# Moving the transposes of the next-but-one pair's k directly behind the narrow matmuls, in a kernel of kernelized attention and a two-layer mixer

## The chip, the cores and the metric

The kernel runs on one core of a Trainium2 chip. The metric is device time in microseconds (us) of one execution. Before the change it is 1147.09 us, the median of three runs (1145.02 to 1147.52).

## The reference

Inputs are q, k and v (8 batches, 8 heads, 576 rows, 64 columns), w_phi (64 x 128), and for the mixer U (576 x 32), V (32 x 576), w_ch1 (512 x 2048) and w_ch2 (2048 x 512).

```python
def phi(x):
    proj = np.einsum('bhsd,df->bhsf', x, w_phi)
    proj = proj - np.max(np.abs(proj), axis=-1, keepdims=True)
    return np.concatenate([np.exp(proj), np.exp(-proj)], axis=-1)
q_p, k_p = (phi(q), phi(k))
kv = np.einsum('bhsf,bhsd->bhfd', k_p, v)
z = np.sum(k_p, axis=2)
num = np.einsum('bhsf,bhfd->bhsd', q_p, kv)
den = np.einsum('bhsf,bhf->bhs', q_p, z)[..., None] + 1e-06
# x = num / den, with heads side by side: (8, 576, 512)
xt = x.transpose(0, 2, 1)
h = xt @ U @ V
u = x + h.transpose(0, 2, 1)
return u + np.maximum(u @ w_ch1, 0.0) @ w_ch2
```

The weights of the mixer come as 64-bit numbers, and the kernel converts them itself.

## The kernel before, in words

**Work.** Attention goes by pairs: two heads of one batch, 32 pairs (b, j) with j = 0 to 3. The 576 rows are four tiles of 128 and a tail of 64; the tails of the two heads, of k and of q, share tiles of their own. For each pair the kernel loads k, q (`raw`, `t_r`) and v (`vb`, `vt`), transposes k and q on TensorE (PE) into PSUM, copies them from there to SBUF, projects them with w_phi, builds the features (maxima and both exponentials), and then does narrow matmuls: kv = features of k times v with a column of ones (L840, L850), and features of q times kv (L870, L877). After the four pairs of a batch, `Tokens` does U and V (`split`, `down`, `up`), and `Mixer` the two wide layers for 512 rows at a time.

**Precision by splitting.** PE works with fp32r operands that are split in a high and a low part. `stack` (L462) does this for the transposed tiles: ScalarE (ACT) copies a half from PSUM to rows 0 to 63 of the tile (`stack_hi`, L468), and VectorE (DVE) writes the remainder to rows 64 to 127 (`stack_lo`, L471). So each transposed tile needs two copies and two subtractions before it is usable, and its PSUM bank is full until then. The narrow matmuls are plain fp32 and use half of the array's columns at a time.

**Filling PE.** The mixer's matmuls are cut into chunks of 12 matmuls of 128x512: `hidden` (L1079) into the one bank of the tag "ph", followed by a relu on ACT (L1095) and its remainder on DVE (L1096), and `add` (L1110) into four banks "o". `mix()` issues the next chunk. Chunks are put between the steps of the pairs, so that PE has work while ACT, DVE and GpSimd (POOL) make features.

**Order.** The first seven pairs and most of the first mixer are issued from a list (`ORDER`), on all engines. From the eighth pair on, the function `ordered` is used. There PE's order is the program's, written by hand (`manual_schedule` for the tensor engine alone), and the other engines' queues are ordered by the framework, from its own simulated clock and the program order. Once fixed, every queue runs in order.

**One pair in `ordered`.** While pair n (`cur`) is finished, pair n+1 (`nxt`) makes its features, and pair n+2 (`far`) is loaded and has its k transposed. In order on PE: k tail and first half (`s_k0`), chunk, second half (`s_k1`, L810), chunk, transposes of q of nxt (L732), chunk, the block of narrow matmuls (`narrow`: `s_out` of cur, `s_kv` of nxt), chunk, tail and first half of q (`s_q0`: L822, L823 into pqt, L831, L832 into pq0), chunk, second half (`s_q1`: L831, L832 into pq1), transposes of k of far (one of the tail, L477, into tT, and four, L732, into T0), and two more chunks. In the last pair of a batch (j = 3) no k is transposed at this place; it is done in `boundary`, between the batches. In j = 1, half of the batch's result is split after the narrow block (`tk.split(0)`, ACT and DVE) and multiplied with U after the transposes (`tk.down(0)`).

**Buffers.** PSUM has eight banks: three with the tag "at" (L145), one "ph", four "o". The "at" banks are taken by pkt, pk, T0, T1, tT, xp0, xp1, kv_ps, pqt, pq0, pq1, pp, vp and pt, whichever comes next, as they come free. In SBUF the transposed tiles live in the pool `att`, which has one buffer for each tag that asks for no more: `tail_T` (L478, for k's tail and q's) and `T` (L735, for k and for q in turn) have one each, feature tiles four. `raw` has two, `t_r` one. A tile's buffer goes to the next tile when all that read or write it is done.

```python
    att = ctx.enter_context(tc.tile_pool(name="att", bufs=1))
    BANKS = {"at": 3, "ph": 1, "o": 4}
    return pT, att.tile([P, 2, SM], F32R, tag="T", name=f"T{n}_{self.nm}")
    self.tail_T = att.tile([P, 2, P], F32R, tag="tail_T", name=f"tail_T{nm}")
```

Of the kernel before, what the change touches and what calls it, by code (L numbers as in the profile page):

```python
# [103 lines left out]
def tile_kernel(  # L104
# [1047 lines left out]
    def mix(n=1):  # L1152
        for _ in range(n):
            if todo:
                fn, f, *ts = todo.pop(0)
                fn(f, *ts)
# [11 lines left out]
    def narrow(nxt, cur, x, xt):  # L1168

        with tc.manual_schedule(engines={nc.tensor.engine}):  # L1170
            cur.s_out(x, xt)
            if nxt is not None:
                nxt.s_kv()
# [108 lines left out]
    def boundary(m, early=None, late=None):  # L1282

        mix(len(todo) - 5)
        if early is not None:
            early(2)
            early(3)
        m.transposes(0)
        mix()
        m.transposes(1)  # L1290
        m.transposes(2)
        mix()
        m.transposes(3)
        mix()
        if early is not None:
            early(NT)
        if late is not None:
            late()
        mix()
        new = m.chunks()  # L1300
        todo.insert(0, new.pop(0))
        todo.extend(new)
        mix()

    def ordered(cur, nxt, x, xt, tk, far):

        for n, (b, j) in list(enumerate(pairs))[ORDERED:]:
            last = j == NPAIR - 1
            if far is None and n + 2 < len(pairs):
                far = Pair(*pairs[n + 2])  # L1310
                far.load_v()

            def do(who, name):
                if who is not None:
                    getattr(who, name)()

            do(nxt, "s_k0")
            mix(2 if j == 0 else 1)
            do(nxt, "s_k1")
            if not last:  # L1320
                mix()
            do(nxt, "transpose_q")
            mix()
            narrow(nxt, cur, x, xt)
            if j == 1:
                tk.split(0)
            if last:
                tk.split(1)
            mix()
            do(nxt, "s_q0")  # L1330
            mix()
            do(nxt, "s_q1")
            if not last:
                do(far, "transpose_k")
                mix()
                if j == 1:
                    tk.down(0)
                mix()
            else:
                mix()  # L1340
                tk.down(1)
                mix()
                tk.up(0)
                tk.up(1)
                mix()
                boundary(Mixer(b, x), tk.up, far.transpose_k if far is not None else None)
                if nxt is not None:
                    if b % 2 == 1:
                        xt = moe.tile([P, C], F32, tag="xt", name=f"xt{b + 1}")
                        nc.vector.memset(xt[ST:P], 0.0)  # L1350
                    x = moe.tile([P, NT, C], F32, tag="x", name=f"x{b + 1}")
                    tk = Tokens(b + 1, x, xt)
            cur, nxt, far = nxt, far, None
        x = moe.tile([P, NT, C], F32, tag="x", name="x_tail")
        nc.sync.dma_start(out=x, in_=u_dram[B])
        boundary(Mixer(B, x))
        mix(len(todo))
# [8 lines left out]
    with tc.manual_schedule(engines={nc.tensor.engine}):  # L1366
        ordered(cur, nxt, x, xt, tk, None)
# [31 lines left out]
```

## Time and profile before

| | |
|---|---|
| median of three runs | 1147.09 us |
| the profiled execution's own time | 1146.92 us |
| its span, first to last instruction | 1145.1 us |
| mean granted clock of TensorE | 0.996 |
| chain that ended last: PE, DVE, DMA, ACT | 91%, 6%, 1%, 1% |
| of it: L1110 (add), L1079 (hidden) | 35%, 33% |
| of it: narrow matmuls L877, L850 | 5%, 5% |

How to read the rows: times are microseconds from the span's start unless marked ns. PE is the matmul, PEld the weight load, which overlaps it; ACT, DVE, POOL and SP are ScalarE, VectorE, GpSimd and the queue that issues DMAs (SPq). L732 is line 732 of the kernel. A row of the timeline has start, duration, engine, line, operation, output and inputs, and how many were merged; in brackets stands how long the engine had been idle and what let it go. A row of a group has the count, the summed time, the mean in ns, and the idle time ahead of it. Matmuls are pipelined: they start every 0.23 us in a chunk although a row shows 0.39 us for one, and their ends are modelled. A window's row has, for each engine, busy us and the number of instructions, then PEclk, the granted clock as a share of full speed.

### The profile page before, as it was taken

The page shows a single profiled execution, that of the slowest core. Times are in us where ns is not written, and L with a number is a line of the kernel's source. Part 1 is how long each engine was busy: PE and PEld are TensorE (multiplying, and loading weights), DVE is VectorE, ACT ScalarE, POOL GpSimd, SP SyncE. Part 2 cuts the span into 40 slices and gives each one's busy share as a digit, 9 for nine tenths or more (in the row PEclk, how much of TensorE's full clock was granted, in tenths as well). Part 3 has the DMA queues.
Part 4 walks back from the last instruction along what each step waited for, and adds up shares of the span by engine and source line. Part 5 has one row for each costly group of instructions (what it writes and reads, how often), then busy time and mean ns, then how long its engine had stood idle before and what let it go on. Part 6 is the DMA issues. An engine that isn't in the chain of part 4 may idle for free.

```text
span 1145.1 us, 22294 instructions
## 1 busy us (share of the span) xinstructions
PE 1124.7 (98%) x9234; PEld 921.2 (80%) x9241; DVE 655.5 (57%) x1355; ACT 525.6 (46%) x1134; POOL 157.4 (14%) x119
## 2 busy tenths in 40 slices
PE   7889999999999999999999999999999999999998
PEld 5775666688888888888888888888888888888886
DVE  7999988856655656655565655665565633112111
ACT  6878876445434544344534544454544521111110
POOL 4321111011111111011201111121101110000000
PEclk9999999999999999999999999999999999999999
DMA  7355533211122112211131112211221005001001
GB/s 195 90 162 174 167 107 121 104 38 32 52 81 69 32 33 76 84 40 33 50 108 32 32 53 73 74 35 32 67 99 32 20 1 171 1 0 38 1 1 37
DMA packets 90532, 75.73 MB, mean 66 GB/s; under 512 B 51648, under 2 KB 76736, under 8 KB 90304
## 3 DMA queue, kind: packets, MB, share of 16 engines
q1 hardware_dynamic: 90112, 73.79, 21.5%
q8 instruction: 73, 1.20, 0.4%
q10 hardware_dynamic: 320, 0.52, 0.1%
q14 instruction: 27, 0.22, 0.1%
HBM read 55.41 MB, written 18.87 MB: 65 GB/s over the span
## 4 chain that ended last, share of the span: by engine, by line
PE 91%; DVE 6%; DMA 1%; ACT 1%; SPq 1%; issue 0%; POOL 0%; DVEq 0%
PE o L1110 35%; PE ph L1079 33%; PE xp L877 5%; PE kv_ps L850 5%; PE pk L810 2%; PE T L732 2%; PE pt L1058 1%; PE pp L969 1%; PE kv_ps L840 1%; PE pq L831 1%; PE xp L870 1%; PE pq L832 1%; PE vp L993 1%; DMA w<-in_moe_w_ch_dram 1%; DVE w_r L240 0%; DVE w_r L243 0%
## 5 line engine op out<-in xcount | busy, mean ns | idle before, releaser
L1079 PE MATMUL ph<-uT_hi,w_hi 128*128 128x512 f32 x576 | 230.9, 401 | 0.0
L1079 PE MATMUL ph<-uT_hi,w_lo 128*128 128x512 f32 x576 | 224.9, 390 | 0.0
L1079 PE MATMUL ph<-uT_lo,w_hi 128*128 128x512 f32 x576 | 224.6, 390 | 0.0
L1096 DVE SCALAR_TENSOR_TENSOR h_lo<-ph,h_hi 128x512 fp32r<-128x512 f32 x128 | 88.1, 689 | 228.8 <-ACT h_hi L1095 228.8
L1110 PE MATMUL o<-w_hi,h_hi 128*128 128x512 f32 x512 | 205.2, 401 | 0.0
L1110 PE MATMUL o<-w_lo,h_hi 128*128 128x512 f32 x512 | 200.1, 391 | 0.0
L1110 PE MATMUL o<-w_hi,h_lo 128*128 128x512 f32 x512 | 200.0, 391 | 0.0
L1095 ACT ACTIVATE h_hi<-ph 128x512 fp32r<-128x512 f32 x128 | 76.5, 598 | 259.1 <-PE ph L1079 258.9
L1079 PEld LDWEIGHTS ph<-uT_hi,w_lo 128*128 128x128 f32 x576 | 108.1, 188 | 23.5
L1079 PEld LDWEIGHTS ph<-uT_hi,w_hi 128*128 128x128 f32 x576 | 108.2, 188 | 22.2 <-issue 0.5
L1079 PEld LDWEIGHTS ph<-uT_lo,w_hi 128*128 128x128 f32 x576 | 108.4, 188 | 21.6 <-issue 0.9
L1110 PEld LDWEIGHTS o<-w_hi,h_lo 128*128 128x128 f32 x512 | 96.1, 188 | 21.0
L1110 PEld LDWEIGHTS o<-w_hi,h_hi 128*128 128x128 f32 x512 | 96.2, 188 | 18.7
L1110 PEld LDWEIGHTS o<-w_lo,h_hi 128*128 128x128 f32 x512 | 96.4, 188 | 17.4
L788 POOL PARTITION_ALL_REDUCE qp_t<-qp_t x24 | 17.8, 740 | 626.8 <-ACT qp_t L787 626.8
L788 POOL PARTITION_ALL_REDUCE qp<-qp x48 | 95.9, 1998 | 32.2 <-ACT qp L787 30.6
L471 DVE TENSOR_TENSOR T<-T,T 64x512 fp32r<-64x512 f32 x96 | 66.2, 689 | 29.6 <-ACT T L468 27.0
L468 ACT CAST T<-T 64x512 fp32r<-64x512 f32 x96 | 55.9, 582 | 36.1 <-PE T L732 19.3
L877 PE MATMUL xp<-kv,qp 128*64 128x65 f32 x2048 | 66.8, 222 | 1.9 <-DVE kv L857 1.5
L850 PE MATMUL kv_ps<-vb,kp 128*64 128x65 f32 x2048 | 66.6, 224 | 0.0
L877 PEld LDWEIGHTS xp<-kv,qp 128*64 128x64 f32 x2048 | 63.1, 138 | 4.1 <-ACT kp L651 2.0
L850 PEld LDWEIGHTS kv_ps<-vb,kp 128*64 128x64 f32 x2048 | 65.7, 140 | 0.0
(156 smaller groups left out, 1564.8 us busy)
## 6 DMA issues: line engine op xcount, KB each, us to landing
w<-in_moe_w_ch_dram SPq DMA_DIRECT2D x32, 512.0 KB, 3.9
raw<-in_q_dram SPq DMA_DIRECT2D x32, 256.0 KB, 2.7
raw<-in_k_dram SPq DMA_DIRECT2D x32, 256.0 KB, 3.0
vb<-in_v_dram SPq DMA_DIRECT2D x64, 128.0 KB, 3.0
u_dram<-x SPq DMA_DIRECT2D x32, 256.0 KB, 2.6
st<-u_dram SPq DMA_DIRECT2D x16, 512.0 KB, 3.8
out_dram<-st SPq DMA_DIRECT2D x32, 256.0 KB, 2.5
t_r<-in_k_dram SPq DMA_DIRECT2D x32, 32.0 KB, 2.2
```

What stands on the lines that cost most here:

```text
L468: nc.scalar.copy(out=dst[0:D], in_=src)
L471: nc.vector.tensor_sub(dst[D:2 * D], src, f32(dst[0:D]))
L732: nc.tensor.transpose(out=pT[:, c * P:(c + 1) * P], in_=self.raw[n][:, c // 2, c % 2, :], identity=ident)
L788: nc.gpsimd.partition_all_reduce(qp[0], qp[1], P, ReduceOp.absmax)
L810: nc.tensor.matmul(pk[:, i, :, :], self.T[0][:, i, cs], w_hl, start=True, stop=True)
L831: nc.tensor.matmul(pq, w_hi, qT, start=True, stop=False)
L850: nc.tensor.matmul(self.kv_v[z * HP:(z + 1) * HP, f, g, :], kp[f][:, i, z * HP:(z + 1) * HP], self.vb[:, g, t, :], start=False, stop=(t == ...
L877: nc.tensor.matmul(xv[zs, c, :], qp[f][:, c * P + z * HP:c * P + (z + 1) * HP], self.kv[:, f, c // 2, :], start=(f == 0), stop=(f == 1), s ...
L1079: nc.tensor.matmul(ph, l[:, c * P:(c + 1) * P], r[:, c, :], start=(n == 0), stop=(n == len(terms) * NCC - 1))
L1095: nc.scalar.activation(out=h_hi, in_=ph, func=AF.Relu)
L1096: nc.vector.scalar_tensor_tensor(out=h_lo, in0=ph, scalar=0.0, in1=f32(h_hi), op0=ALU.max, op1=ALU.subtract)
L1110: nc.tensor.matmul(self.o[t], l[:, cs], r, start=(f == 0 and n == 0), stop=(f == NFC - 1 and n == len(terms) - 1))
```

## The change

In `ordered`, the transposes of `far`'s k are issued directly behind the narrow block instead of behind the second half of q, that is, two chunks earlier, ahead of `s_q0` and `s_q1`. This holds for j = 0, 1 and 2; the last pair of a batch, which has them in `boundary`, is not changed. No instruction is added or left out, and all sizes and buffers stay.

```diff
             do(nxt, "transpose_q")
             mix()
             narrow(nxt, cur, x, xt)
+            if not last:
+                do(far, "transpose_k")
             if j == 1:
                 tk.split(0)
             if last:
@@ -1331,7 +1333,6 @@
             mix()
             do(nxt, "s_q1")
             if not last:
-                do(far, "transpose_k")
                 mix()
                 if j == 1:
                     tk.down(0)
```

## The prediction

> **What bounds the kernel now.** I read the page first, then busy time by windows, then the waits, and then the timeline around one move of the transposes.
>
> ```profile
> span 1145.1 us, 22294 instructions
> PE 1124.7 (98%) x9234; PEld 921.2 (80%) x9241; DVE 655.5 (57%) x1355; ACT 525.6 (46%) x1134; POOL 157.4 (14%) x119
> ```
>
> TensorE (PE) is busy for 98% of the span, so it is the engine to watch. An average can hide a stage with another limit, so the second view is busy time in windows: a gap early on, the stretch behind that gap, and the ordered part.
>
> ```profile
> core 0: us, PE busy (x) PEld busy (x) DVE busy (x) ACT busy (x) POOL busy (x), PEclk, DMA share, GB/s
> 195.60:198.50 2.90, 0.40 (x2) 0.00 (x0) 2.84 (x6) 2.14 (x4) 0.00 (x0) 1.00 0.31 90
> 198.50:203.40 4.90, 4.89 (x9) 2.26 (x10) 4.83 (x9) 2.98 (x5) 0.00 (x0) 0.65 0.76 270
> 221.00:947.00 726.00, 726.00 (x6405) 618.27 (x6404) 418.66 (x877) 335.35 (x751) 107.68 (x69) 1.00 0.17 51
> ```
>
> The change touches only the ordered part, and there (221 to 947 us) PE is busy for 726.00 of 726.00 us at the full granted clock. No other engine sets the end. So only two things count: what an instruction costs in PE's own stream, and whether PE, whose order is written by hand, now meets a wait that it doesn't meet today. Each of either adds directly to the time.
>
> **How often.** Transposes of k are issued 23 times by this function:
>
> ```profile
> L477 PE MATMUL tT<-ident,t_r 128*128 128x128 f32 x23 | 6.2, 270 | 0.0
> ```
>
> Six of these stand in the boundaries (tokens 1 to 6) and do not move. The 17 others move: three pairs in each of tokens 2 to 6, and j = 0 and 1 in token 7, where j = 2 has no next-but-one pair.
>
> **Removed at the old place.** The timeline of PE, first with the transposes behind the second q projection, then one pair later (j = 3), where they do not stand there:
>
> ```profile
> 422.35 0.39 PE L832 MATMUL pq<-T,w_hl 128*128 128x512 f32 x1
> 422.58 0.27 PE L477 MATMUL tT<-ident,t_r 128*128 128x128 f32 x1
> 422.69 0.60 PE L732 MATMUL T<-ident,raw 128*128 128x128 f32 x4
> ...
> 425.88 0.39 PE L1079 MATMUL ph<-uT_hi,w_hi 128*128 128x512 f32 x1
> ```
> ```profile
> 446.86 0.39 PE L832 MATMUL pq<-T,w_hl 128*128 128x512 f32 x1
> ...
> 449.81 0.76 PE L969 MATMUL pp<-xs,u_all 128*128 128x256 f32 x5
> ```
>
> From the last projection matmul to the end of the following chunk of 12 matmuls it is 425.88 − 422.35 = 3.53 us with the five transposes and 449.81 − 446.86 = 2.95 us without. The old place costs 0.58 us each, 17 × 0.58 = 9.9 us.
>
> **Added at the new place.** The trace has transposes directly behind narrow matmuls, early on; beside them stands the place where they will be put:
>
> ```profile
> 67.24 3.44 PE L850 MATMUL kv_ps<-vb,kp 128*64 128x65 f32 x64
> 70.60 1.10 PE L1058 MATMUL pt<-ident,x 128*128 128x128 f32 x8
> ```
> ```profile
> 259.92 2.04 PE L850 MATMUL kv_ps<-vb,kp 128*64 128x65 f32 x64
> 261.89 0.50 PE L1079 MATMUL ph<-uT_hi,w_hi 128*128 128x512 f32 x1
> ...
> 264.76 0.22 PE L822 MATMUL pqt<-tail_T,w_hl 128*128 128x128 f32 x1
> ```
>
> A transpose starts 0.08 us before the modelled end of the narrow block (70.68), a chunk 0.07 us before it (261.96): the way out of the narrow block costs both the same. Eight transposes start within 1.10 − 0.27 = 0.83 us. In the four above, starts are (0.60 − 0.27)/3 = 0.11 apart, so the first gap is 0.17 us and the fifth transpose starts 0.17 + 3 × 0.11 = 0.50 us behind the first. From a fifth transpose (423.02) to the end of the chunk behind it is 425.88 − 423.02 = 2.86 us. The stretch from the narrow block to the tail's q projection so becomes 0.50 + 2.86 = 3.36 us where it is 264.76 − 261.89 = 2.87 us: +0.49 us each, 17 × 0.49 = 8.3 us. The move alone is worth 8.3 − 9.9 = −1.6 us: one change of matmul kind less in each pair.
>
> **The wait that comes with it.** Transposed k needs two PSUM banks (tT, T0) and goes by ScalarE (ACT) and VectorE (DVE) into the SBUF tiles T and tail_T. The pool `att` gives each of these tags one buffer. At the old place the current pair's q has left both. At the new place it has not: T still holds the transposed q, which L831 and L832 read, and tail_T its tail, read by L822 and L823. A new user of a buffer waits for its last reader, as the loads of the raw tiles show in SP's waits:
>
> ```profile
> SPq L434 <- PE T L732: 207.6, 23, 12.2
> ```
>
> So the copies out of T0's bank cannot start before the second q projection, and those out of tT's bank not before the tail's. Only three banks carry the tag "at". Two stay full over the next chunk, and pqt, pq0 and pq1 must share the third. The projections pqt and pq0 stand back to back: pq0 now waits until ACT has copied pqt out. pq1 comes a chunk later and finds a free bank. Today's rows, first a pair with an add chunk in front, then one with a hidden chunk (j = 1):
>
> ```profile
> 418.77 0.28 PE L823 MATMUL pqt<-tail_T,w_hl 128*128 128x128 f32 x1
> 419.09 0.27 ACT L787 COPY qp_t<-pqt 128x128 f32<-128x128 f32 x1 [7.12 <-PE pqt L823]
> 419.17 0.39 PE L832 MATMUL pq<-T,w_hl 128*128 128x512 f32 x1
> ```
> ```profile
> 264.96 0.60 ACT L1095 ACTIVATE h_hi<-ph 128x512 fp32r<-128x512 f32 x1 [2.85 <-PE ph L1079]
> 265.21 0.39 PE L832 MATMUL pq<-T,w_hl 128*128 128x512 f32 x1
> 265.45 0.26 ACT L787 COPY qp_t<-pqt 128x128 f32<-128x128 f32 x1
> ```
>
> And how soon PE starts once another engine lets it go:
>
> ```profile
> 198.03 0.42 DVE L982 TENSOR_TENSOR pst<-pp,pst 32x256 fp32r<-32x256 f32 x1
> 198.51 0.73 PE L993 MATMUL vp<-pst,v_all 128*128 128x512 f32 x2 [2.51 <-DVE pst L982]
> ```
>
> PE starts 198.51 − 198.45 = 0.06 us after the release, and the second matmul starts 0.73 − 0.39 = 0.34 us after the first, since nothing hides the weight load. With an add chunk in front the copy ends at 419.36, so L832 starts at 419.36 + 0.06 + 0.34 = 419.76 instead of 419.17: 0.59 us of stall. With a hidden chunk in front ACT does the relu first, the copy ends at 265.71, and L832 starts at 266.11 instead of 265.21: 0.90 us. Eleven of the 17 pairs (j = 0 and 2) are of the first kind, six (j = 1) of the second: 11 × 0.59 + 6 × 0.90 = 11.9 us.
>
> That is the low end. The tail's stacking becomes ready at the same moment as the pqt copy and stands earlier in the program, so ACT may take its first copy ahead. How ACT's stacking runs today:
>
> ```profile
> 297.84 0.26 ACT L468 CAST tail_T<-tT 64x128 fp32r<-64x128 f32 x1
> 298.00 0.59 ACT L468 CAST T<-T 64x512 fp32r<-64x512 f32 x1
> ...
> 298.24 0.28 DVE L471 TENSOR_TENSOR tail_T<-tT,tail_T 64x128 fp32r<-64x128 f32 x1
> 298.62 0.26 ACT L468 CAST tail_T<-tT 64x128 fp32r<-64x128 f32 x1
> ```
>
> An ACT instruction behind the small copy starts 0.16 us after it (298.00 − 297.84). Put ahead of pqt, that adds 17 × 0.16 = 2.7 us: the high end is 14.6 us. No row says which ACT takes, so I take the middle, 13.2 us.
>
> **What hides the rest.** The banks of xp0 and xp1 should be free when the transposes come: the last DVE read of xp1, in the tightest kind of pair (j = 1), ends at 261.36, the narrow block at 261.96. The bank of kv_ps is free before pqt.
>
> ```profile
> 260.94 0.42 DVE L892 TENSOR_TENSOR x<-xp,den 128x256 f32<-128x256 f32 x1
> ...
> 262.50 0.42 DVE L857 COPY kv<-kv_ps 128x260 f32<-128x260 f32 x1
> ```
>
> T must be full before the next pair's k projection, two chunks (over 5 us) behind pq1. Its stacking still starts at the end of pq1, as today, and two halves of 0.59 and about 0.7 us each fit twice. The transposes issue no DMA, but they free t_r and the raw k buffer, whose next loads are on SP:
>
> ```profile
> 422.88 0.62 SPq L446 DMA_DIRECT2D t_r<-in_k_dram  x1
> 423.60 0.55 SPq L434 DMA_DIRECT2D raw<-in_k_dram  x1
> 424.20 0.62 SPq L446 DMA_DIRECT2D t_r<-in_q_dram  x1
> ```
>
> These would issue some 6 us earlier, among the loads of v, and be needed some 25 us later: nothing. POOL gets q's maxima under a microsecond later, about 20 us before use: nothing.
>
> **The sum**, against the profiled execution's 1146.92 us (span 1145.1 and 1.8 around it; it lies 0.2 us under the median 1147.09): 1146.92 − 1.6 + 13.2 = 1158.5 us. Its own range, by the two ends of the stall, is 1157.2 to 1159.9.
>
> **Rivals.**
> 1. *No wait at pq0 (not slower).* If the stacking could leave the banks within the chunk behind the transposes, which takes a second buffer for T and tail_T, pq0 would find a bank and only the −1.6 us of the move would stay: 1145.3 us. It decides as soon as tT's bank is free before pqt ends. For it: the chunk is 2.86 us long, and ACT is idle (7.12 us in the row of 419.09). Against it: one buffer for each tag. Chance 0.09.
> 2. *pq0 gets tT's bank instead of pqt's.* Then it waits for the whole chain of the tail: copy, subtract, copy, subtract, with starts 0.40 and 0.38 apart in the rows at 297.84, and so 0.40 + 0.38 + 0.40 + 0.28 = 1.46 us in place of a copy of 0.27. The stalls become 1.78 and 2.10 us, in all 32.2: 1146.9 − 1.6 + 32.2 = 1177.5 us. Against it: pqt's bank is free first, whoever goes first on ACT. Chance 0.06.
> 3. *The transposes wait too.* xp1's read has a margin of 0.6 us in the six j = 1 pairs, and there DVE also has the split's subtractions. One such operation ahead costs up to 0.42, 2.5 us in all. If T0 had to take the bank of kv_ps, whose copy ends at 262.92, it would start at 262.98 instead of 261.89 + 0.17: 0.92 × 6 = 5.5 us. 1161 to 1164 us. Chance 0.06.
> 4. *The stalls cost clock.* The gap of 2.51 us before 198.51 was followed by 4.90 us at a granted clock of 0.65, a loss of 0.35 × 4.9 = 1.7 us. If each of the 17 stalls did that: 1158.5 + 29 = 1187.5 us. Against it: PE's weight loads sit idle ahead of the narrow blocks 22 times, 0.35 us on average, and the ordered part has PEclk 1.00.
>
> ```profile
> PEld xp L870 <- issue: 7.6, 22, 0.4
> ```
>
> The stalls are between the two sizes, nearer the small one: chance 0.03. The Trainium skill has this rule ("TensorE: Matmul & The Clock Gate", section "A second HAM failure mode: psum-queue depth-cycling"): waiting on PSUM banks can idle PE briefly and so often that its clock swings between half and full. By that rule the trace agrees for the long gap and not for the short ones.
>
> **How the numbers follow.** The stall at pq0 has 0.76: 1158.5 us. The range must leave out no more than 0.2; without rivals 1, 2 and 4 it leaves out 0.18. Its low end: the stall is 0.59 in all 17 pairs if ACT copies pqt ahead of the relu, 10.0 − 1.6 gives 1155.3, and 0.05 us of misreading each gives 1154. Its high end is rival 3 on top of 1159.9: 1166. A measurement of this kernel can tell about 0.2%, 2.3 us, from no change; rival 1, at −0.14%, lies inside that but for a little. Faster 0.02, same 0.08, slower 0.90.
>
> **What would show it.** In the changed profile: a gap of 0.4 to 1.1 us on PE ahead of L831 in 17 pairs, released by ACT's L787 of qp_t, longer for j = 1; L477 right behind L850; tail_T's L468 behind L823, T's L468 behind the second L832; no new wait at L477 or L732. Wrong it would be if L831 still follows L823 within 0.2 us (rival 1), if the releaser is DVE's L471 (rival 2), if L732 waits (rival 3), or if PEclk falls below 1 in the ordered part (rival 4).

## The result, and the profile after

The changed kernel takes 1158.4 us (median of four runs, 1157.66 to 1159.31) against 1147.01 us for the kernel before in the same session: a ratio of 1.0106, with a 95% interval of 1.0093 to 1.0118. It is slower by 11.4 us. The profiled execution took 1159.31 us. The page after, then the window of the ordered part:

```profile
span 1157.5 us, 22310 instructions
...
PE 1127.6 (97%) x9234; PEld 923.4 (80%) x9241; DVE 661.4 (57%) x1355; ACT 523.6 (45%) x1134; POOL 155.7 (13%) x119
```
```profile
core 0: us, PE busy (x) PEld busy (x) DVE busy (x) ACT busy (x) POOL busy (x), PEclk, DMA share, GB/s
221.00:959.60 738.60, 728.05 (x6406) 619.64 (x6406) 424.49 (x878) 333.45 (x751) 106.73 (x69) 1.00 0.17 50
```

PE has the same number of matmuls as before and the full clock, but it is idle for 738.60 − 728.05 = 10.55 us of a stage in which it had no idle time. The waits of PE, and of its weight loads, say who ended that time:

```profile
PE pq L831 <- ACT qp_t L787: 10.5, 17, 0.8
```
```profile
PEld pq L831 <- ACT qp_t L787: 12.9, 17, 1.0
```

Neither line was there before, and the 17 waits are those of the 17 pairs whose transposes moved. L831 writes pq0, and L787 of qp_t is ACT's copy out of pqt. The idle time on PE understates the wait: in the pair below, L831 starts 0.79 us behind L823 where it was 0.11, but PE counts as idle for 0.51 us only, since the row of L823 covers the rest. Here is one pair with an add chunk in front, PE, ACT and DVE together:

```profile
234.20 0.52 PE L850 MATMUL kv_ps<-vb,kp 128*64 128x65 f32 x12
...
234.65 0.33 PE L477 MATMUL tT<-ident,t_r 128*128 128x128 f32 x1
...
234.81 0.60 PE L732 MATMUL T<-ident,raw 128*128 128x128 f32 x4
...
238.07 0.28 PE L823 MATMUL pqt<-tail_T,w_hl 128*128 128x128 f32 x1
238.38 0.26 ACT L468 CAST tail_T<-tT 64x128 fp32r<-64x128 f32 x1 [7.59 <-PE pqt L823]
238.55 0.26 ACT L787 COPY qp_t<-pqt 128x128 f32<-128x128 f32 x1
238.68 0.28 DVE L471 TENSOR_TENSOR tail_T<-tT,tail_T 64x128 fp32r<-64x128 f32 x1 [3.49 <-ACT tail_T L468]
...
238.86 0.50 PE L831 MATMUL pq<-T,w_hl 128*128 128x512 f32 x1 [0.51 <-ACT qp_t L787]
```

The transposes stand directly behind the narrow block and wait for nothing. ACT had been idle for 7.59 us although the tail has lain transposed in its bank since 235: its copy is let go by L823, the last reader of the old tail_T. ACT then takes the tail's copy ahead of that of pqt, and PE goes on 0.05 us after the end of the second (238.81). The same place in a pair with a hidden chunk in front, where the relu comes first as well:

```profile
265.98 0.28 PE L823 MATMUL pqt<-tail_T,w_hl 128*128 128x128 f32 x1
266.12 0.60 ACT L1095 ACTIVATE h_hi<-ph 128x512 fp32r<-128x512 f32 x1 [3.33 <-PE ph L1079]
266.61 0.25 ACT L468 CAST tail_T<-tT 64x128 fp32r<-64x128 f32 x1
...
266.76 0.27 ACT L787 COPY qp_t<-pqt 128x128 f32<-128x128 f32 x1
267.08 0.19 PEld L831 LDWEIGHTS pq<-T,w_hl 128*128 128x128 f32 x1 [0.96 <-ACT qp_t L787]
267.08 0.50 PE L831 MATMUL pq<-T,w_hl 128*128 128x512 f32 x1 [0.82 <-ACT qp_t L787]
...
267.42 0.40 PE L832 MATMUL pq<-T,w_hl 128*128 128x512 f32 x1
```

From L823 to L832 it is now 267.42 − 265.98 = 1.44 us here and 1.13 us in the other kind (L832 at 239.20), where it was 0.40 in both: stalls of 1.04 and 0.73 us.

**A sharper ruler.** Medians of one kernel scatter by a microsecond or more, and in the profiles most of that lies ahead of the ordered part. There the granted clock is not the same in each: its mean from 0 to 232 us is 0.99 in the profile before, 0.98 in the one after, and from 0.98 to 1.00 in the runs below. So the runs below are compared by the stretch of PE from the kv matmuls that start at about 232 us to the last L877. Before and after, from the timeline and from the line of that group (its first and last start):

```profile
232.18 0.61 PE L840 MATMUL kv_ps<-vt,kp_t 128*64 128x130 f32 x8
```
```profile
L877 PE MATMUL xp<-kv,qp x2048: 220/222/271, 24.7 to 937.4; 128*64 128x65 f32 x187
```
```profile
232.24 0.61 PE L840 MATMUL kv_ps<-vt,kp_t 128*64 128x130 f32 x8
```
```profile
L877 PE MATMUL xp<-kv,qp x2048: 220/222/316, 25.0 to 949.9; 128*64 128x65 f32 x187
```

Before it is 937.4 − 232.2 = 705.2 us, after 949.9 − 232.2 = 717.7 us: +12.5 us. Within a profile the time from one pair's kv matmuls to the next pair's repeats to 0.02 us from batch to batch.

### The profile page after: what moved, and what is told of

Same layout as the page of the kernel before. It is cut to its first block, busy times and chain, and to the rows that moved or that the text cites. A ratio compares the mean times of both kernels' runs of the same rounds, so it can differ in the third digit from the quotient of the medians.

```text
span 1157.5 us, 22310 instructions
## 1 busy us (share of the span) xinstructions
PE 1127.6 (97%) x9234; PEld 923.4 (80%) x9241; DVE 661.4 (57%) x1355; ACT 523.6 (45%) x1134; POOL 155.7 (13%) x119
## 4 chain that ended last, share of the span: by engine, by line
PE 90%; DVE 5%; ACT 2%; DMA 1%; SPq 1%; issue 0%; POOL 0%; DVEq 0%
PE o L1110 34%; PE ph L1079 33%; PE xp L877 5%; PE kv_ps L850 5%; PE pk L810 2%; PE T L732 2%; PE pt L1058 1%; PE pp L969 1%; PE pq L831 1%; PE kv_ps L840 1%; PE xp L870 1%; PE pq L832 1%; PE vp L993 1%; DMA w<-in_moe_w_ch_dram 1%; DVE w_r L243 0%
## 5 line engine op out<-in xcount | busy, mean ns | idle before, releaser
L471 DVE TENSOR_TENSOR T<-T,T 64x512 fp32r<-64x512 f32 x96 | 66.2, 689 | 45.2 <-ACT T L468 43.2
L877 PE MATMUL xp<-kv,qp 128*64 128x65 f32 x2048 | 68.1, 224 | 1.9 <-DVE kv L857 1.5
L877 PEld LDWEIGHTS xp<-kv,qp 128*64 128x64 f32 x2048 | 64.4, 140 | 4.1 <-ACT kp L651 2.0
```

The source lines that it names most:

```text
L471: nc.vector.tensor_sub(dst[D:2 * D], src, f32(dst[0:D]))
L877: nc.tensor.matmul(xv[zs, c, :], qp[f][:, c * P + z * HP:c * P + (z + 1) * HP], self.kv[:, f, c // 2, :], start=(f == 0), stop=(f == 1), s ...
```

## The experiments

Three theories were held against each other. A, that of the prediction: two of the three "at" banks stay full, so pq0 must wait for the copy of pqt. B: the order on ACT is what PE waits for, the tail's copy ahead of that of pqt. C: transposes behind the narrow block are dear in PE's own stream. In the table, the ordered stretch is that of one profile of each kernel, against 705.2 us; the ratio is of the runs' times against those of the kernel before in the same session.

| run | ordered stretch | ratio, 95% interval | waits at pq0 |
|---|---|---|---|
| the change | +12.5 us | 1.0106 (1.0093 to 1.0118) | 17 |
| only the four transposes of T0 moved | −1.3 us | 0.9991 (0.9982 to 0.9999) | none |
| only the tail's transpose moved | −0.9 us | 0.9988 (0.9979 to 0.9997) | none |
| tail stacked later in the program | +10.6 us | 1.0095 (1.0082 to 1.0108) | 17 |
| second buffer for the tail (14 pairs moved) | −1.5 us | 0.9996 (0.9986 to 1.0005) | none |
| moved in j = 1 alone | +5.5 us | 1.0050 (1.0037 to 1.0062) | 6 |
| moved, pqt early | +0.1 us | 1.0013 (1.0003 to 1.0022) | none; 5 waits at pqt |
| pqt early alone | +1.8 us | 1.0032 (1.0021 to 1.0042) | none; 5 waits at pqt |
| moved, pqt early in j = 0, 1, 2 | −2.3 us | 0.9976 (0.9968 to 0.9985) | none |
| pqt early in j = 0, 1, 2 alone | −0.6 us | 0.9991 (0.9982 to 1.0000) | none |

**Only the four transposes of T0 moved.** `transpose_k` is cut in two; the tail's half stays at the old place.

```diff
             narrow(nxt, cur, x, xt)
             if not last:
-                do(far, "transpose_k")
+                do(far, "transpose_k_main")
...
             do(nxt, "s_q1")
             if not last:
+                do(far, "transpose_k_tail")
```

> Only the four transposes of T0 stand behind the narrow block; the tail's one (tT) stays behind the second q projection. Theory A: one bank stays full over the chunk, pqt and pq0 have the two others, no wait at L831. Move alone: old place 0.58 - 4 x 0.11 = 0.14 us left there, 0.49 - 0.11 = 0.38 us added, 0.06 us less for each of 17: -1.0 us against the kernel before. Rival B: the same. Rival C: four fifths of +11.4 stay, +9 us.

The wait is gone (pq0's first matmul starts 0.11 us behind pqt's last in all pairs, as in the kernel before), and the stretch is 1.3 us shorter than before. With one bank full there is one for pqt and one for pq0. This speaks against C, which left 9 us.

**Only the tail's transpose moved.** The two halves change places.

> Only the tail's transpose (tT) stands behind the narrow block; the four of T0 stay behind the second q projection. Theory A: again one bank is full, so no wait at L831, about -1.0 us against the kernel before, though ACT still takes the tail's first copy ahead of that of pqt. Rival B: ACT's order is as in the changed kernel, so the wait stays, 17 stalls of 0.73 or 1.04 us, +13 us. Rival C: a fifth of +11.4, +2.3 us.

The stretch is 0.9 us shorter than before, and this run tells A from B. The row order on ACT is that of the changed kernel, the tail's copy ahead of that of pqt, and yet PE does not wait (the new functions put the lines 12 further down: L835 is L823, L843 is L831, L799 is L787):

```profile
236.75 0.28 PE L835 MATMUL pqt<-tail_T,w_hl 128*128 128x128 f32 x1
...
236.87 0.45 PE L843 MATMUL pq<-T,w_hl 128*128 128x512 f32 x1
...
237.07 0.26 ACT L468 CAST tail_T<-tT 64x128 fp32r<-64x128 f32 x1 [7.14 <-PE pqt L835]
...
237.23 0.26 ACT L799 COPY qp_t<-pqt 128x128 f32<-128x128 f32 x1
```

pq0 starts at 236.87, ahead of both copies. Each half of the move alone is harmless; only both together, which fill two banks, bring the wait. B as the cause is out.

**The tail stacked later in the program.** The transposes stay behind the narrow block, but the calls that copy out of tT and T0 stand behind `s_q0` and `s_q1`.

```diff
             narrow(nxt, cur, x, xt)
             if not last:
-                do(far, "transpose_k")
+                do(far, "transpose_k_pe")
...
             do(nxt, "s_q0")
+            if not last:
+                do(far, "transpose_k_tail")
             mix()
             do(nxt, "s_q1")
             if not last:
+                do(far, "transpose_k_T")
```

> The changed kernel, but the copies out of tT and T0 stand in the program behind the steps s_q0 and s_q1 instead of ahead, so ACT should take the copy of pqt first. Transposes and banks as in the changed kernel. Theory A: pq0 still waits for the copy of pqt, 0.16 us less in each of 17 pairs (0.59 and 0.90 us instead of 0.73 and 1.04): 2.4 to 2.7 us under the changed kernel, +8.9 us over the one before. Rival B: the wait goes, -1.8 us against the kernel before. Rival C: as the changed kernel, +11.4 us.

Lines are 20 further down here (L843 is L823, L807 is L787, L851 and L852 are L831 and L832):

```profile
PE pq L851 <- ACT qp_t L807: 7.9, 17, 0.7
```
```profile
237.87 0.28 PE L843 MATMUL pqt<-tail_T,w_hl 128*128 128x128 f32 x1
238.18 0.27 ACT L807 COPY qp_t<-pqt 128x128 f32<-128x128 f32 x1 [7.59 <-PE pqt L843]
238.34 0.26 ACT L468 CAST tail_T<-tT 64x128 fp32r<-64x128 f32 x1
...
238.50 0.53 PE L851 MATMUL pq<-T,w_hl 128*128 128x512 f32 x1 [0.35 <-ACT qp_t L807]
```

ACT now takes pqt first, and PE still waits 17 times, each time shorter: L851 starts 0.63 us behind L843, where L831 started 0.79 us behind L823. So ACT's order is a part of the price, 0.16 us each, and not the cause. The stretch became shorter by 1.9 us and not by the expected 2.4 to 2.7; the last section comes back to that.

**A second buffer for the tail.** SBUF has no free KB for it in all tokens, but from token 3 on one buffer of the split weights is unused. The pairs of token 2 keep the old place.

```diff
-            self.tail_T = att.tile([P, 2, P], F32R, tag="tail_T", name=f"tail_T{nm}")
+            if self.b > SPLIT and self.par == 1:
+                t = const.tile([P, C], F32R, tag=f"wl{2 * NFC}", name=f"tail_T{nm}")
+                self.tail_T = t[:, 0:2 * P].rearrange("p (a b) -> p a b", a=2)
+            else:
+                self.tail_T = att.tile([P, 2, P], F32R, tag="tail_T", name=f"tail_T{nm}")
```

> From token 3 on, the tails of odd pairs go to a second SBUF buffer, so far's tail can be stacked at once; the 14 pairs of tokens 3 to 7 have the transposes behind the narrow block, the three of token 2 keep the old place. Theory A (banks: two of three stay full, so pq0 waits for the copy of pqt): tT's bank comes free within the chunk, pq0 finds a bank, no wait at L831, and only the gain of the move is left, 14 x -0.11 = -1.5 us: 0.13% below the kernel before. Rival B (ACT's queue: the tail's first copy ahead of that of pqt is what PE waits for): the same, since the tail is stacked earlier. Rival C (transposes behind narrow matmuls are dear in PE's own stream): 14/17 of +11.4 stay, +9.4 us.

The rows of a pair in token 3 show the tail leaving its bank within the chunk (lines are 4 further down: L827 is L823, L835 is L831):

```profile
359.02 0.33 PE L477 MATMUL tT<-ident,t_r 128*128 128x128 f32 x1
...
359.38 0.26 ACT L468 CAST tail_T<-tT 64x128 fp32r<-64x128 f32 x1 [4.22 <-PE tT L477]
...
360.29 0.29 DVE L471 TENSOR_TENSOR tail_T<-tT,tail_T 64x128 fp32r<-64x128 f32 x1 [0.33 <-ACT tail_T L468]
...
362.44 0.28 PE L827 MATMUL pqt<-tail_T,w_hl 128*128 128x128 f32 x1
...
362.56 0.45 PE L835 MATMUL pq<-T,w_hl 128*128 128x512 f32 x1
```

ACT starts on the tail right behind its transpose and no longer waits for pqt, and tT's bank has been read out at 360.58, nearly 2 us before pqt. The stretch is 1.5 us shorter, as A worked it out, with the same transposes at the new place and no wait. So what kept tT's bank full is the one SBUF buffer behind it, and the move alone is worth 0.11 us a pair. T was given no second buffer: here too its copy out of T0 starts only behind the second half of q, so one bank stays full, which does no harm. In the runs' times the gain can't be told from no change.

**Moved in j = 1 alone.** The eleven other pairs keep the old place.

> Only the six pairs with j = 1 have the transposes behind the narrow block, the eleven others keep the old place. Theory A with the relu as part of the price: six stalls of 1.04 us less six times the move's 0.09 = +5.7 us in the ordered part. If all 17 pairs cost the same (12.5 / 17 = 0.74 us each): +4.4 us. If only the add-chunk pairs paid: -0.6 us.

+5.5 us, 0.92 us for each of the six pairs. They cost more than the others, and in their rows above it is the relu that ACT does ahead of the copies, so the relu is a part of the price. The eleven others then paid (12.5 − 5.5) / 11 = 0.64 us each.

**pqt early.** If tail_T is to be free sooner without a second buffer, its last reader has to come sooner. The tail's q projection needs only tail_T, so it can stand a chunk ahead of the narrow block.

```diff
             do(nxt, "transpose_q")
+            do(nxt, "project_q_tail")
             mix()
             narrow(nxt, cur, x, xt)
...
         def s_q0(self):
-            self.project_q_tail()
```

> The changed kernel, and the tail's q projection (pqt) is issued a chunk ahead of the narrow block, behind the transposes of q, instead of right ahead of pq0. No buffer is added. tail_T is then free when far's tail is transposed, so tT's bank empties within the chunk, and pqt's own bank is long free. Theory A: no wait at L831 in any of the 17 pairs, 17 x -0.11 = -1.8 us in the ordered part against the kernel before, 14 us under the changed kernel. If the wait came from the order of ACT alone (rival B): the same. If something else of the move were dear (rival C): +11 us stay.

> The kernel before, with only the earlier tail's q projection of the run beside it. Theory A: nothing waited in the kernel before, so the earlier projection alone gains nothing, within 0.5 us; what the run beside it gains is the move's. If the earlier projection has a gain of its own, -1 us or more.

The waits at pq0 went, but the gain did not come: in both runs pqt has a wait of its own in the last pair of a batch. In the run with the move:

```profile
PEld pqt L822 <- DVE kp L814: 3.0, 6, 0.6
```

In j = 3 no chunk stands between the second k projection and the transposes of q. pk10, pk11 and T1 fill the three banks, and pqt waits until DVE has read one of them (L814). Five of the six waits lie in the ordered stretch, one ahead of it. The control has the same six and is 1.8 us longer in the ordered stretch, so the expectation that the early pqt costs nothing was wrong. By the medians the control is slower by about 4 us in all. The rest lies ahead of the ordered part: in its profile the kv matmuls that stand at 232.18 before are at 235.53. From 60 to 100 us its granted clock is 0.91, and 0.96 before, which makes up to 40 × 0.05 = 2 us by an estimate; the cause of what is left stays open.

**pqt early where there is room.** pqt stays at its old place in j = 3.

```diff
-            do(nxt, "project_q_tail")
+            if not last:
+                do(nxt, "project_q_tail")
             mix()
             narrow(nxt, cur, x, xt)
...
+            if last:
+                do(nxt, "project_q_tail")
             do(nxt, "s_q0")
```

> As the run with pqt a chunk ahead of the narrow block and the transposes moved, but pqt stands early in the pairs j = 0, 1 and 2 alone; in j = 3 it is where it was, since there it met three full banks behind the second k projection and waited 0.39 us. Theory A: no wait left in the ordered part; 17 x -0.11 = -1.8 us there against the kernel before, -14.3 us against the changed kernel. Rival C (something else of the move is dear): over the kernel before.

> The kernel before with only pqt early in j = 0, 1 and 2: the ordered part within 0.5 us of the kernel before, so that what the run beside it gains is the move's alone. What comes before the ordered part may differ by a microsecond or two, as it did between profiles of the other runs.

With the transposes moved it takes 1144.67 us against 1147.03 us, 0.9976 (0.9968 to 0.9985): faster than the kernel before by 0.24%, which is more than the measurement's uncertainty. Its ordered part is without idle time on PE:

```profile
232.50:934.00 701.50, 701.50 (x6199) 599.17 (x6197) 407.96 (x847) 326.89 (x734) 105.98 (x68) 1.00 0.18 52
```

Of the 2.3 us in the stretch, the control has 0.6; the move, freed of its wait, brings 1.7. Of the control's 0.6 us, 0.23 us are no gain: the first early pqt stands ahead of the kv matmuls with which the stretch begins, and so drops out of it. This is so in all four runs with pqt early.

## Why the prediction was right, step by step

- *PE sets the end in the ordered part.* Right: stalls of PE went straight into the time, as the sum below shows.
- *The move alone, −1.6 us.* Right: −1.5 us for 14 pairs with the second buffer, −1.7 us for 17 with pqt early, so −0.10 to −0.11 us each where −0.09 was worked out. The new place costs a little less than the 0.49 us of the prediction: in the changed kernel's pair with j = 1 it is 265.92 − 262.58 = 3.34 us from L477 to L822, where the prediction put 3.36.
- *The wait at pq0.* Right in place, count and releaser. That it takes two full banks was shown by filling only one of them, and what keeps tT's bank full by giving the tail a second buffer. That it is ACT's order (a way to read the same wait) fell.
- *Its size.* The term was put at 13.2 us, the middle of 11.9 and 14.6. It measured 11 × 0.73 + 6 × 1.04 = 14.3 us: ACT does take the tail's copy first, so the high end was the right one. The order on ACT, which the prediction found in no row of the profile before, was worth 17 × 0.16 = 2.7 us. The terms of one stall held: PE goes on 0.05 us after the release (0.06 in the prediction), and L832 starts 0.34 us behind L831.
- *The sum.* In the ordered part 14.3 − 1.8 = 12.5 us, 0.9 us above the forecast sum of 11.6. The medians came out 11.4 us apart, nearer to the forecast than its own terms. That 1158.4 us was measured where 1158.5 was forecast is luck: the terms were off by 0.9 us, and single runs of the kernel before lie up to 2.5 us apart (1145.02 to 1147.52).
- *What hides the rest.* Right. L477 and L732 wait for nothing; the raw k and t_r loads are issued within about 3 us behind the narrow block, and nobody waits for them.
- *Rivals.* 1 would have kept L831 within 0.2 us of L823; it starts 0.79 us behind. 2 would have DVE's L471 as the releaser; it is ACT's L787. 3 would show a wait at L732. 4 would show in PEclk, which is 1.00 in the ordered part with 17 gaps of 0.5 to 0.8 us, the nearest two of them 28 us apart. The Trainium skill's rule that frequent short gaps for PSUM banks make the clock swing ("TensorE: Matmul & The Clock Gate", section "A second HAM failure mode: psum-queue depth-cycling") is not seen at this size and spacing. The gap that the prediction held beside them is of another kind, a wait for DVE and not for a bank (L982 of pst), and far longer: in the profile before, the clock is 0.50 from 199.95 to 203.37 us, and in the 3.41 us ahead of that PE was busy for 1.44 us. A gap of 0.8 us leaves 2.6 of 3.4 us busy.

## What to carry to other kernels

A step moved ahead of another doesn't only bring its own instructions; here it also held its PSUM banks from the moment it wrote them until the SBUF buffer behind them was free and the copies were done. So before moving a producer ask who last reads the SBUF tile that its result goes to. If two matmuls in a row need a bank each, count the banks that are full at that point: with one left, the copy of the first stood on TensorE's path in all 17 pairs, and with two left in none. The cure with the largest gain needed no more memory, only an earlier last reader, put where banks are free; moving only one half of the transposes also avoided the wait. What any of them gains over the kernel before is small, 2.4 us of 1147 at most.

## What had not been expected of the hardware

With ACT's order turned, each wait at pq0 became 0.155 us shorter, but in the pairs with an add chunk in front only 0.09 us of it stayed. In the pair at 365 us, the two matmuls of pq0 and the hidden chunk behind them together take 0.07 us longer than in the changed kernel (0.598 + 2.767 against 0.572 + 2.725 us, start to start): matmuls that start 0.227 us apart there are 0.23 to 0.24 apart here for most of the chunk. In the pairs with j = 1 the full 0.16 us stayed. From one pair's kv matmuls to the next it is 27.85 us where the changed kernel has 27.93 (j = 0), and 29.27 where it has 29.43 (j = 1). Nothing in the profile shows a wait at that place, the granted clock of the ordered part is 1.00 in both, and it was not tried further; its cause stays open.
